# Attention and a squared-ReLU FFN in one program: other PSUM banks for the third pair of output tiles, and two small steps on other engines

## The chip, the cores and the metric

The program runs on one core of one Trainium2 chip. The metric is device time in microseconds (us), and less is better. Before the change three runs took 420.18, 419.59 and 418.35 us; their median, 419.59 us, is the time before. A core has a matrix engine (TensorE: PE for its matmuls, PEld for its weight loads), a vector engine (VectorE, DVE), an engine for activation functions (ScalarE, ACT), GpSimd (POOL), and SyncE (SP), which only issues transfers here. PSUM, where matmuls accumulate, has 8 banks of 512 float32 per partition.

## The reference

```python
def _attn_ref(q, k, v):          # q (8,16,384,64), k and v (8,4,384,64)
    ...
    scores = scale * np.matmul(q, k.transpose(0, 1, 3, 2))
    ...
    attn = np.exp(scores)
    attn = attn / (np.sum(attn, axis=-1, keepdims=True) + 1e-09)
    return np.matmul(attn, v).astype(np.float32)

def _moe_ref(x, w_in, w_out):    # x (3072,1024), w_in (1024,2048), w_out (2048,1024)
    h = np.maximum(x @ w_in, 0.0)
    return (h * h @ w_out).astype(np.float32)
```

The attention output of each batch element, 384 tokens by 16 heads of 64, is the input of the FFN for those 384 rows. Four query heads share a key head.

## The kernel before

The work goes through 8 batches (b = 0 to 7) of 384 tokens. A batch has five stages.

- **Scores** (L392): for a key block and a group of four heads, K times Q into two neighbouring banks; ScalarE takes the exponential of both banks in one instruction (L402, some 1.0 us).
- **AV** (`av`, L418, for the first three batches; `av_halves`, L459, after that): the exponentials are the weights and V is the moving operand. V carries one more column, `ones_b` of `v_aug`, so that the row sum comes out beside the product; VectorE takes a reciprocal and multiplies (L427/L433, L472/L474). From b = 2 that column holds a scale instead of 1, and `v_unit` (L622) writes it from `tops`, the largest magnitude of V, which is found in `top_of` (L601, a reduce on VectorE and a copy to `top_w` on GpSimd, L603) and `top_spread` (L613, two matmuls and a reduce, L617). An AV step reads that column and waits for it.
- **Turning**: the result is transposed to `xT`, from b = 1 by a DMA that SP issues (`turn_o_dma`, L479).
- **Up**: x times w_in. For b = 0 and 1 plain tiles: `up_tile`, or `quad`, which works on four 128-row tiles in banks 4 to 7, in two phases of two banks for each half of the contraction. A tile goes to `hr` through a relu on VectorE (L567) and is squared into `h2T` by ScalarE (L571) or VectorE (L574). From b = 2 (`strassen`) up is made of seven products of quarter matrices, 14 `units` of two tiles' width each; units sit in a pair of banks, 4 and 5 or 6 and 7, in turn. It needs sums of w_in's quarters (`w_q`: `fold` L636, `scaled` L648, `less` L653, `w_in_place` L662 and L666), made once on VectorE during b = 0 and 1, and sums of xT's quarters (`sums`, L593), made for each batch. `evict` copies or adds a unit into `hr` (L777, L782, L769) and `close_squares` picks engines for relu and square (L687, L690, L693, L697).
- **Down**: h2T times w_out into 384 x 1024. `down_halves` (b = 2 to 7, matmuls at L847) works on pairs of tiles: `p` is rows 0 (both column halves), `q` rows 1 and `r` rows 2. The contraction is cut in halves for partitions 0-63 and 64-127, which run on the two row halves of TensorE at once; the second list runs one item (four matmuls of each half) behind the first. `p` has banks 4 and 5, `q` 6 and 7, `r` 2 and 3. The order of items is p0-p3, q0 q1, p4-p7, q2 q3, r0 r1, then q and r in turn, then r4-r7. The last batch has no `r`; its rows 2 are plain tiles (`downs`, L903) in bank 6 or 7. `store` evicts a tile on VectorE (L924, or L920 for b = 0 and 1) and SP issues the transfer out.

While down of batch b runs, AV of batch b + 1 is threaded between its items, in bank pairs (0, 1) and (2, 3), and then, "beside" it, the first scores of b + 2 in banks 0 and 1. While up of b + 1 runs, the rest of these scores follow ("split"). `top_spread` also takes one of the pairs.

The order on each engine is written down before anything runs. A `Recorder` keeps a clock per engine, in its own estimates (`cost`), and a loop (L1099 to L1277) always takes, among the candidates (scores, AV, FFN items and others), what its clocks call ready, by priority. Every engine then executes its own list in that order and waits on semaphores. A bank is free for the planner when its last reader is done; `held` marks banks whose tile is still open. Work on one engine waits behind what was recorded earlier on it. Four things on GpSimd's list matter below: the loads of q, k and v two batches ahead (L239, L271, L264), which wait until the transposes of the previous q are done; `dup_k` (L300); the copy of V (`aug_v`, L305); and L603. For a batch from 3 on, `dup_k`, the copy and `top_of` are put on the lists only when the scores of the batch before are all on the list.

Names used below for lines: relu of a quad L567, its squares L571 and L574, v's scale column L622, third pair `r` in `down_halves`.

## Time and profile before

| what | us |
|---|---|
| median of three runs | 419.59 |
| the profiled execution | 418.33 |
| its span, from the first to the last instruction | 416.4 |
| PE busy | 405.7 (97%) |
| PEld busy | 292.6 (70%) |
| DVE busy | 275.2 (66%) |
| ACT busy | 203.4 (49%) |
| POOL busy | 100.3 (24%) |
| granted TensorE clock | 1.000 |

The profile comes from one execution, 418.33 us long; 416.4 us of it lie between its first and its last instruction. In a timeline a row gives the start in us from the beginning of the span, the time it covers, the engine, the line, the operation, what it writes and reads, the number of merged instructions, and in brackets how long the engine had been idle just before and what ended that. A row of PE can overlap the next, because the end of a matmul is modelled and matmuls are pipelined; the distance of two starts is the safer figure. Up, scores and down of the first batch take until about 73 us, the second batch until about 127 us, and from there a batch takes about 49 us.

### The profile page before, as it was taken

To read this page: it belongs to the slowest core of one execution; us is meant where nothing else is said; L and a number is where in the kernel's file an instruction comes from. 1 tells how busy PE (TensorE), PEld (TensorE's weight loads), DVE (VectorE), ACT (ScalarE), POOL (GpSimd) and SP (SyncE) were. 2 spreads that over 40 slices of the span, in tenths; PEclk is the share of its full clock that TensorE was granted. 3 is DMA by queue.
4 is the path that set the end of the run, shared out by engine and by line. 5 is a ranking of instruction groups with operands and counts; after the bars stand their busy time and mean duration, and the time that the engine had idled before them with its cause. 6 is when DMAs were issued, how large, how long until landed. Compare 5 with 4: busy or idle time off the path is not lost.

```text
span 416.4 us, 14931 instructions
## 1 busy us (share of the span) xinstructions
PE 405.7 (97%) x6873; PEld 292.6 (70%) x6880; DVE 275.2 (66%) x525; ACT 203.4 (49%) x279; POOL 100.3 (24%) x115
## 2 busy tenths in 40 slices
PE   8999999999899999999999999999999999999997
PEld 5566754554467975488965998569985789779844
DVE  3699988899787765457644684367834577456613
ACT  6948610186007970477605963269613785006500
POOL 8680000141400923009200363005300060002200
DMA  9999999992991079520991148930734201521012
GB/s 172 190 191 193 205 187 177 259 115 64 182 164 52 3 115 140 115 93 14 169 176 54 54 54 122 178 110 3 91 68 90 102 3 22 91 73 52 3 50 102
DMA packets 96943, 44.75 MB, mean 107 GB/s; under 512 B 77296, under 2 KB 90864, under 8 KB 96880
## 3 DMA queue, kind: packets, MB, share of 16 engines
q0 software_dynamic: 36544, 17.44, 33.3%
q1 hardware_dynamic: 59664, 25.86, 31.2%
q8 instruction: 54, 0.88, 0.9%
q10 hardware_dynamic: 672, 0.49, 0.4%
q14 instruction: 9, 0.07, 0.1%
HBM read 35.65 MB, written 12.58 MB: 116 GB/s over the span
## 4 chain that ended last, share of the span: by engine, by line
PE 82%; DVE 9%; ACT 2%; DMA 2%; issue 2%; POOL 1%; SPq 1%; POOLq 0%; DVEq 0%
PE ps L847 27%; PE ps L798 25%; PE ps L903 7%; PE ps L392 7%; PE ps L554 5%; PE ps L459 5%; PE ps L418 3%; ACT expT L402 2%; DMA qT<-q_st 1%; PE ps L517 1%; DVE hr L567 1%; DVE hr L777 1%; DVE wx L648 1%; DVE wx L653 1%; DMA wx<-in_k_dram 1%
## 5 line engine op out<-in xcount | busy, mean ns | idle before, releaser
L402 ACT ACTIVATE expT<-ps 128x1024 bf16<-128x1024 f32 (+1 forms) x145 | 139.4, 1028 | 113.7 <-PE ps L392 113.1
L847 PE MATMUL ps<-w_out_sb,h2T 64*128 64x512 bf16 x1088 | 140.3, 376 | 0.8 <-issue 0.2
L847 PEld LDWEIGHTS ps<-w_out_sb,h2T 64*128 64x128 bf16 x1088 | 64.9, 94 | 37.9 <-issue 0.7
L798 PE MATMUL ps<-xT,w_in_sb 64*128 64x192 f16 x1152 | 82.5, 243 | 0.2 <-DVE xT L593 0.2
L798 PEld LDWEIGHTS ps<-xT,w_in_sb 64*128 64x128 f16 x1152 | 71.8, 94 | 5.0 <-PE ps L798 1.2
L690 POOL TENSOR_SCALAR hr<-hr 128x384 f32<-128x384 f32 x18 | 28.2, 1565 | 183.0 <-DVE hr L782 183.0
L924 DVE TENSOR_SCALAR y_sb<-ps,unit 128x512 f32<-128x512 f32 (+2 forms) x37 | 29.3, 794 | 36.2 <-PE ps L847 30.3
L798 PE MATMUL ps<-s_sum,wx 64*128 64x192 f16 x768 | 51.1, 243 | 0.8
L392 PE MATMUL ps<-qT,kT 64*128 64x256 bf16 (+2 forms) x336 | 50.6, 324 | 0.9 <-ACT expT L402 0.7
L903 PE MATMUL ps<-w_out_sb,h2T 128*128 128x512 bf16 (+2 forms) x233 | 48.6, 364 | 0.7 <-DVE y_sb L924 0.3
L782 DVE TENSOR_TENSOR hr<-ps,hr 128x384 f32<-128x384 f32 x72 | 39.6, 556 | 14.5 <-PE ps L798 11.7
L798 PEld LDWEIGHTS ps<-s_sum,wx 64*128 64x128 f16 x768 | 44.0, 94 | 4.2 <-DVE hr L777 2.8
L777 DVE COPY hr<-ps 128x384 f32<-128x384 f32 x64 | 34.9, 556 | 13.7 <-PE ps L798 9.7
L459 PEld LDWEIGHTS ps<-v_aug,expT 64*128 64x128 bf16 x1440 | 37.2, 94 | 8.8 <-DVE tops L617 0.9
L554 PE MATMUL ps<-xT,w_in_sb 64*128 64x384 bf16 x448 | 42.1, 323 | 0.7 <-DVE hr L567 0.6
L903 PEld LDWEIGHTS ps<-w_out_sb,h2T 128*128 128x128 bf16 x240 | 22.4, 98 | 25.1 <-DVE y_sb L924 0.5
L459 PE MATMUL ps<-v_aug,expT 64*128 64x65 bf16 x1440 | 37.4, 190 | 1.3 <-issue 0.6
L554 PEld LDWEIGHTS ps<-xT,w_in_sb 64*128 64x128 bf16 x448 | 21.4, 94 | 16.7 <-DVE hr L567 1.8
L798 PE MATMUL ps<-s_sum,w_in_sb 64*128 64x192 f16 x384 | 32.9, 243 | 0.1
L693 ACT ACTIVATE h2T<-hr 128x384 bf16<-128x384 f32 x62 | 31.6, 521 | 1.7
L798 PE MATMUL ps<-xT,wx 64*128 64x192 f16 x384 | 31.8, 243 | 0.1
L687 ACT ACTIVATE hr<-hr 128x384 f32<-128x384 f32 x54 | 27.7, 513 | 7.6 <-DVE hr L782 7.6
(85 smaller groups left out, 410.7 us busy)
## 6 DMA issues: line engine op xcount, KB each, us to landing
out_dram<-y_sb SPq DMA_DIRECT2D x47, 256.0 KB, 2.3
q_st<-in_q_dram POOLq DMA_DIRECT2D x12, 384.0 KB, 7.9
w_in_sb<-in_moe_w_in_dram POOLq DMA_DIRECT2D x8, 512.0 KB, 14.8
w_out_sb<-in_moe_w_out_dram POOLq DMA_DIRECT2D x4, 1024.0 KB, 28.5
v_st<-in_v_dram POOLq DMA_DIRECT2D x7, 192.0 KB, 8.4
k_st<-in_k_dram POOLq DMA_DIRECT2D x6, 192.0 KB, 4.7
wx<-in_q_dram POOLq DMA_DIRECT2D x2, 384.0 KB, 7.9
q_st<-in_q_dram POOLq DMA_DIRECT2D x3, 192.0 KB, 5.3
```

What stands on the lines that cost most here:

```text
L392: mm = pe.matmul(ps[:, base + x, m * wide:(m + 1) * wide], kT[at(b)][64 * x:64 * x + 64, u, :], q_cols(b, u // NJ, x, c0, c0 + wide))
L402: R.add("scalar", lambda e: e.activation(dst, src, AF.Exp, scale=0.125), reads=keys, writes=[("expT", (b * NU + u) % NEX, t) for u, _, _ i ...
L459: m = pe.matmul(ps[:, p[x], n * DP:n * DP + D + 1], w, v_aug[b % 2][r, g * NJ + j, 0:D + 1], start=(n + j + y == 0), stop=(n + j + y == 2 ...
L554: m = pe.matmul(bank(4 + xs[x])[:, 0:S], w_in_sb[r, kc, c * 128:(c + 1) * 128], xT[b % NXT][r, kc, :], start=(phase < 2 and kc == 0), stop ...
L690: R.add("gpsimd", lambda e, val=val: e.tensor_scalar(val, val, DOWN * DOWN, 0.0, ALU.mult, ALU.max), reads=[("hr", r)], writes=[("hr", r)] ...
L693: R.add("scalar", lambda e, dst=dst, two=two: e.activation(dst, two, AF.Square), reads=[("hr", r)], writes=keys, cost=0.45)
L777: R.add("vector", lambda e: e.tensor_copy(hr[r][:, :], src), reads=[("bank", at)], writes=[("hr", r)], cost=0.48, after=hr_read.pop(r, ()))
L782: R.add("vector", lambda e: e.tensor_tensor(hr[r][:, :], src, hr[r][:, :], ALU.add), reads=[("bank", at), ("hr", r)], writes=[("hr", r)], ...
L798: return lambda pe: pe.matmul(bank(at)[:, f * h:f * h + h], w[r, kc, c:c + 128], m[r, kc, :], start=(prod in (1, 5, 2) and y + f + kc == 0 ...
L847: return lambda pe: pe.matmul(bank(base + x)[:, 0:512], h2T[r, c, i3 * 128:(i3 + 1) * 128], w_out_sb[r, c, x * 512:(x + 1) * 512], start=( ...
L903: m = pe.matmul(bank(i)[:, 0:n], h2T[:, c, i3 * 128:(i3 + 1) * 128], w_out_sb[:, c, c0:c1], start=(c == 0), stop=(c == NFC - 1))
L924: R.add("vector", lambda e: e.tensor_scalar(ysl, bank(i)[:, 0:n], g, g, ALU.mult, ALU.mult), reads=[("bank", i), ("unit", b % 2)], writes= ...
```

## The change

1. The third pair `r` of `down_halves` no longer has banks 2 and 3. It uses the banks of the first pair, after that has been evicted. Which pair of banks is the first one alternates by batch: banks 4 and 5 for an even batch, 6 and 7 for an odd one; `q` has the other pair.
2. The banks of the Strassen units alternate by batch in the same way.
3. `v_unit` (L622) is recorded on VectorE in place of GpSimd.
4. In a quad of batch 1 a square may go to GpSimd: when ScalarE's clock is not well behind TensorE's, and GpSimd's clock plus 0.3 is before VectorE's, with 1.0 added while sums of w_in are still to be made.
5. The planner's estimate for a `fold` is 1.14 in place of 1.2, and inside a split stage of a batch outside 2 to 6 the second half of an AV step may be taken.

```diff
 # in quad, after the relus
                 for c, r in rs if phase == 3 else ():
-                    if R.clock["scalar"] < R.clock["tensor"] - 0.5:
+                    pool, dve = [max(R.clock[x], R.clock["tensor"] + 0.5) for x in ("gpsimd", "vector")]
+                    if b == 1 and R.clock["scalar"] >= R.clock["tensor"] - 0.5 and pool + 0.3 < dve + 1.0 * bool(w_q):
+                        R.add("gpsimd", lambda e, c=c, r=r: e.tensor_tensor(h2T[:, c, :], hr[r][:, :], hr[r][:, :], ALU.mult),
+                              reads=[("hr", r)], writes=[("h2T", c, 0), ("h2T", c, 1)], cost=0.77)
+                    elif R.clock["scalar"] < R.clock["tensor"] - 0.5:
...
 # in v_unit
-        R.add("gpsimd", lambda e: e.tensor_scalar(ones_b, tops[b % 2].ap().unsqueeze(1).to_broadcast([128, NU, 1]),
+        R.add("vector", lambda e: e.tensor_scalar(ones_b, tops[b % 2].ap().unsqueeze(1).to_broadcast([128, NU, 1]),
                                                   TINY, DOWN, ALU.max, ALU.mult),
-              reads=[("tops", b % 2)], writes=[("v_one", b % 2)], cost=0.15)
+              reads=[("tops", b % 2)], writes=[("v_one", b % 2)], cost=0.12)
...
 # in fold
-              reads=[("w_in", i)], writes=[("w_top", n)], cost=1.2)
+              reads=[("w_in", i)], writes=[("w_top", n)], cost=1.14)
...
 # in strassen
-        units = [(prod, 2 * g + i, 4 + (2 * (n % 2 ^ g) + i)) for g in range(2)
+        units = [(prod, 2 * g + i, 4 + (2 * (n % 2 ^ g ^ b % 2) + i)) for g in range(2)
                  for n, prod in enumerate((1, 5, 6, 3, 7, 2, 4)) for i in range(2)]
...
 # in down_halves
-        p, q, r = pair(0, 4), pair(1, 6), pair(2, 2)
+        lead, other = 4 + 2 * (b % 2), 6 - 2 * (b % 2)
+        p, q, r = pair(0, lead), pair(1, other), pair(2, lead)
...
 # in the planner's loop
-            inside = [x for x in cand if x[2] in ("sc", "ffn") or late and (x[2] == "av2" or x[2] == "av" and since >= AMONG * (1 + (ff["b"] >= SB)))]
+            inside = [x for x in cand if x[2] in ("sc", "ffn") or x[2] == "av2" and not on_halves(ff["b"]) or late and (x[2] == "av2" or x[2] == "av" and since >= AMONG * (1 + (ff["b"] >= SB)))]
```

8 lines of the change are left out of this document (4 added, 4 removed).

## The prediction

> **What bounds the kernel now.** I read the busy shares first, then the table of windows, then the chain that ended last, then the timeline wherever TensorE was idle. TensorE is busy 405.7 of 416.4 us, and the chain is 82% PE. So the change can only win back stretches in which PE waits. By windows of 20 us:
>
> ```profile
> 80.00:100.00 20.00, 19.20 (x232) 10.82 (x228) 18.40 (x31) 15.61 (x17) 5.86 (x7) 1.00 0.69 123
> 100.00:120.00 20.00, 18.45 (x213) 10.61 (x213) 16.28 (x32) 1.53 (x2) 5.42 (x7) 1.00 1.15 178
> 240.00:260.00 20.00, 19.77 (x476) 17.75 (x472) 13.17 (x30) 10.18 (x19) 9.52 (x12) 1.00 0.66 89
> ```
>
> The columns after the length are PE, PEld, DVE, ACT, POOL. The second batch (73 to 127 us) loses most, with VectorE nearly full; the steady batches lose 0.2 to 0.6 us in 20. In the quads of the second batch:
>
> ```profile
> 86.63 1.47 POOL L300 COPY k_dup<-k_st 128x1536 bf16<-128x1536 bf16 x1 [0.66 <-DMA k_st<-in_k_dram]
> 86.70 3.21 DVE L574 TENSOR_TENSOR h2T<-hr 128x384 bf16<-128x384 f32 x4
> 91.16 1.01 DVE L567 TENSOR_SCALAR hr<-ps 128x384 f32<-128x384 f32 x2
> 92.22 1.09 PEld L554 LDWEIGHTS ps<-xT,w_in_sb 64*128 64x128 bf16 x16 [0.56 <-DVE hr L567]
> 94.29 0.82 PE L554 MATMUL ps<-xT,w_in_sb 64*128 64x384 bf16 x8 [0.37 <-DVE hr L567]
> 100.30 3.40 PE L903 MATMUL ps<-w_out_sb,h2T 128*128 128x512 bf16 x15 [0.16 <-DVE hr L567]
> ```
>
> PE waits for relus that stand on VectorE's list behind four squares or a sum of w_in. At 111.8 us PE waits for the scale column of V, which stands on GpSimd's list behind loads that wait for a transpose:
>
> ```profile
> 109.65 1.31 POOL L271 DMA_DIRECT2D q_st<-in_q_dram  x1 [2.67 <-DMA qT<-q_st]
> 110.95 0.76 POOL L264 DMA_DIRECT2D v_st<-in_v_dram  x1
> 111.78 1.56 POOL L622 TENSOR_SCALAR v_aug<-tops 128x12 bf16<-128x12 f32 x2
> 113.02 4.55 PE L418 MATMUL ps<-v_aug,expT 128*128 128x65 bf16 x144 [1.28 <-POOL v_aug L622]
> ```
>
> In a steady batch (here b = 2) the seams are these: AV steps run back to back because the third pair can't open while AV holds banks 2 and 3; then the third pair is evicted as the next up begins.
>
> ```profile
> 164.56 1.74 PE L459 MATMUL ps<-v_aug,expT 64*128 64x65 bf16 x72
> 166.40 1.04 PE L847 MATMUL ps<-w_out_sb,h2T 64*128 64x512 bf16 x8
> ...
> 178.89 1.69 DVE L924 TENSOR_SCALAR y_sb<-ps,unit 128x512 f32<-128x512 f32 x2 [2.21 <-PE ps L847]
> ...
> 180.13 0.24 PE L798 MATMUL ps<-s_sum,wx 64*128 64x192 f16 x1
> ```
>
> And near the end, the last rows wait for a bank of `q`:
>
> ```profile
> 406.00 1.67 DVE L924 TENSOR_SCALAR y_sb<-ps,unit 128x512 f32<-128x512 f32 x2 [1.78 <-PE ps L847]
> 407.09 6.89 PE L903 MATMUL ps<-w_out_sb,h2T 128*128 128x512 bf16 x47 [0.28 <-DVE y_sb L924]
> ```
>
> **Squares on GpSimd.** By starts, PE loses 0.30 us before 92.23 (two score matmuls last 0.21, the step took 0.51), 0.53 before 94.29 (0.75 against 0.22) and 0.33 before 100.30: 1.16 us behind VectorE. Another 0.47 before 99.75 is behind ScalarE's exponentials, which run nearly without a break. The edit's comparison decides by the planner's clocks. The first quad should send two or three squares to GpSimd (one is ScalarE's); the second none, since the planner has GpSimd's four loads wait for the q transposes then; the third and fourth all four. I count 11. VectorE is rid of 11 times 0.49 us (four took 1.95 at 100.21), 5.4 us. GpSimd gets 11 times 0.83 (its L697 of the same shape), 9.1 us, and was busy 5.86 of 20. These squares stand ahead of the next k duplication, V copy and L603, which are recorded after the last scores: the duplication moves from 86.6 to about 101, and SP's transposes and the loads after them two to three us later. Nobody needs them before the scores at 127.0, a cover of over 10 us. The duplication's move also takes away one delay: the first of the four squares at 86.70 lasted 1.80 us, against 0.55 elsewhere. If the relus are on time, ScalarE's 18 exponentials (0.95 each, from 82.2) end the stage near 99.5 in place of 100.6. I take 1.2 us off, out of 1.63 at most; the other end is the first rival.
>
> The row first: that square began on VectorE while GpSimd's copy was running, and ended 0.4 us after the copy. The Trainium skill, page "SBUF — State Buffer", section "Who interferes with whom", says that a VectorE instruction with two SBUF inputs, or in a two-port mode, and a GpSimd instruction that reads SBUF exclude each other, the later one blocked fully. By that rule the squares on GpSimd would hold up the sums of w_in in the same way; the trace agrees at 86.70, yet at 193.02 a VectorE square beside GpSimd's L690 took its usual 0.55. What it would make of the sum is the first rival.
>
> **Scale column on VectorE.** A VectorE instruction on one column (L596) took 0.21 us; six cost 1.2 us, where VectorE is busy 13 of 20. Behind L617 (104.35 to 104.83) it adds no wait, for the AV that last read that column is two batches old, so AV of batch 2 can start near 105 instead of 113.02, and the 1.28 us go. What is late next there: the banks, free since the scores. I take 1.3, between 0.8 (AV held up by its own evictions, eight times 0.75 on VectorE against 4.55 on PE, with sums of w_in in between) and 1.3.
>
> **Start of batch 2's up.** PE started L798 at 127.80, 0.4 us after its four score matmuls, waiting for sums of xT that were queued behind the last sums of w_in. With AV eight us earlier and VectorE relieved, both are done sooner: 0.4 off. SP's four transposes of this AV then queue behind the three of the next q and k, and have some 10 us to land in.
>
> **Third pair.** Gain: AV halves that alternate with down items take 0.28 us each (163.42 to 163.70); four from 164.56 to 166.40 took 1.84, so 0.72 is lost. Likewise 0.55 at 214.44 and at 312.88 (three halves in 1.39 and 1.40), 0.44 at 263.35 without an instruction stall there: 2.3 in all. Cost one: `r` opens one item (0.86 us) after the first pair's last matmul, and that pair's second eviction ends one eviction (0.81) and a handoff of some 0.1 later, unless VectorE is at an AV's 0.75 just then. Between 0 and 0.8 for each of five batches; 0.06, since AV halves lie between, 0.3 in all. Cost two: the second product of the next up wants the banks of `r`. Here it began at 180.13, the second eviction ended at 180.58: 0.5 each. Scores can fill 0.3 of it (banks 2 and 3 are free then; a burst is 0.21), except ahead of the last batch: four times 0.2 and 0.5 is 1.3. Of the gain I take 1.3, because the pair's own last halves stay back to back. Net 0.3 lost, between 2.3 gained and 6.5 lost.
>
> **Other edits.** For the last batch `q` has banks 4 and 5, and the plain tiles find 6 and 7 evicted since 403.4: of the 0.54 us by which the start at 407.09 is late I take 0.4. The fold estimate: four folds took 4.59 us, 1.15 each, so the new value is nearer, at no cost. The half-AV rule: no AV is open in a split stage of batches 0 and 1 here, nothing.
>
> **Sum.** 1.2 + 1.3 + 0.4 + 0.4 - 0.3 = 3.0. The profiled execution would go from 418.33 to 415.3. It stands 1.26 under the median of the runs; by that median, 419.59 - 3.0 = 416.6 us.
>
> **Rivals.**
> 1. *GpSimd's squares hold up VectorE.* Between 78 and 100 VectorE still has some seven sums of w_in. If each waits a whole square, 7 x 0.83 = 5.8 us, more than the 5.4 of relief: no gain in the quads, and the sums late for batch 2. 416.6 + 1.2 + 0.4 = 418.2. For it, the 1.80 us square; against it, the planner puts sums between squares of different quads, and GpSimd is idle in most of that time.
> 2. *The seams eat the gain.* If each of the five costs 0.6 more than I took, 3.0 us: 419.6. For it, evictions in pairs of 1.7 us on VectorE at each seam; against it, spare scores and AV halves.
> 3. *Slower, by the third pair.* At its full price, 0.8 at `r` and 0.5 at the next up, with nothing to fill: 5 x 1.3 = 6.5, and no gain from AV. The rest gains 3.3: 419.6 + 3.2 = 422.8. It decides from 0.66 a batch; from 1.1 it shows.
> 4. *The seams are free.* All 2.3 gained, nothing paid: 416.6 - 2.6 = 414.0. Against it, up's second product wants the bank that is evicted last.
> That squares hardly go to GpSimd (its planned clock late in three quads) would cost most of the 1.2 and is inside the range.
>
> **Numbers.** What this kernel's runs can tell from no change is about 0.5%, 2.1 us, so faster means under 417.5 and slower over 421.7. Forecast 0.50 (its own range 415.3 to 417.5: 0.3 to 0.5 us on each of the four larger terms, not all one way), rival 1 0.10, rival 2 0.18, rival 3 0.10, rival 4 0.12. Faster: 0.50 + 0.12 = 0.62; same: 0.28; slower 0.10. The range from 413.6 to 420.3 leaves out rival 3 and some of the edges of 2 and 4.
>
> **What would show it.** No PE wait on L622; L418 for batch 2 near 105 in one block; L697-like squares on GpSimd between 79 and 102 and few L574 after 90, none much over 0.55 us; no idle time before L903 at the end. Wrong if PE waits on L924 ahead of L847 or L798 at five seams for more than 0.6 us each, if L653 or L648 lengthen beside GpSimd's squares, or if the new order puts a wait where none was.

## The result, and the profile after

The changed kernel takes 421.31 us (median of 20 runs, 417.67 to 426.03) against 418.43 us before in the same comparison (20 runs, 417.27 to 420.20): 1.0055 times as long, with a 95% interval of 1.0033 to 1.0077. It is slower; the forecast was 416.6 us. One thing must be known to read the numbers below: 11 of these 20 runs have a mean granted TensorE clock of 0.996 or less, which only 3 of the 90 runs of the kernel before in the comparisons further down have, and these eleven average 422.75 us where the nine at 1.0 average 419.54, so besides a run's time its clock is told where it matters. At clock 1.0 alone the change costs about 1.1 us, and the rest of the 2.9 us comes with the lower clock. The execution that was profiled took 419.88 us at clock 1.0, with a span of 418.1 us; the one before took 418.33 us, span 416.4.

TensorE is busy 403.4 us (405.7 before) in a longer span, and GpSimd 123.2 us (100.3). The table of windows, with the columns PE, PEld, DVE, ACT, POOL behind the length:

```profile
80.00:100.00 20.00, 18.90 (x230) 10.66 (x224) 19.01 (x26) 16.23 (x18) 13.61 (x14) 1.00 0.73 134
100.00:120.00 20.00, 17.98 (x207) 10.55 (x211) 17.79 (x31) 0.90 (x1) 10.51 (x10) 1.00 0.84 124
120.00:140.00 20.00, 18.05 (x249) 13.15 (x249) 9.75 (x19) 10.06 (x12) 2.19 (x2) 1.00 0.69 116
140.00:160.00 20.00, 17.85 (x429) 15.61 (x427) 13.91 (x29) 14.70 (x23) 11.72 (x12) 1.00 0.30 54
...
240.00:260.00 20.00, 19.87 (x505) 18.29 (x501) 14.79 (x32) 12.21 (x23) 11.08 (x12) 1.00 0.50 73
```

The steady window at 240 has gained 0.10 us of PE (19.77 before). The loss lies between 80 and 160: PE is 0.30, 0.47, 1.76 and 1.58 us less busy there than before (19.20, 18.45, 19.81, 19.43). VectorE was to be relieved in the quads; it is busier (19.01 against 18.40), and GpSimd has gone from 5.86 to 13.61. Between 140 and 160 PE stands twice, where before it has one wait, of 0.45 us:

```profile
146.01 0.50 PE L802 MATMUL ps<-s_sum,wx 64*128 64x192 f16 x8 [0.87 <-DVE hr L781]
...
157.16 0.21 PE L617 MATMUL ps<-ident,top_w 64*128 64x64 bf16 x2 [1.28 <-POOL top_w L607]
```

The second of these is met again in the experiment on the scale column; the first was not followed further.

What PE waits for is in the timeline. Rows of the engines GpSimd, VectorE, PE and SP, in order of time, from the quads of batch 1 to the first up product of batch 2:

```profile
89.00 1.23 DVE L657 TENSOR_TENSOR wx<-wx 128x2048 f16<-128x2048 f16 x1
...
90.77 4.60 POOL L572 TENSOR_TENSOR h2T<-hr 128x384 bf16<-128x384 f32 x4 [4.03 <-DVE hr L567]
...
91.07 1.60 DVE L657 TENSOR_TENSOR wx<-wx 128x2048 f16<-128x2048 f16 x1
...
97.73 5.14 POOL L572 TENSOR_TENSOR h2T<-hr 128x384 bf16<-128x384 f32 x4 [2.36 <-DVE hr L567]
...
98.04 1.60 DVE L657 TENSOR_TENSOR wx<-wx 128x2048 f16<-128x2048 f16 x1
...
100.39 0.81 PE L908 MATMUL ps<-w_out_sb,h2T 128*128 128x512 bf16 x3 [0.88 <-POOL h2T L572]
...
102.82 1.46 POOL L300 COPY k_dup<-k_st 128x1536 bf16<-128x1536 bf16 x1
...
104.23 1.82 POOL L305 COPY v_aug<-v_st 128x768 bf16<-128x768 bf16 x1
104.31 1.29 SPq L309 DMA_TRANSPOSE kT<-k_dup  x1
...
105.64 3.73 SPq L316 DMA_TRANSPOSE qT<-q_st  x2
...
106.00 0.28 POOL L607 CAST top_w<-top 128x128 bf16<-128x128 f32 x1
...
106.34 0.20 PE L617 MATMUL ps<-ident,top_w 64*128 64x64 bf16 x2 [1.53 <-POOL top_w L607]
...
109.42 5.09 SPq L479 DMA_TRANSPOSE xT<-o_sb  x2
...
113.62 0.88 POOL L271 DMA_DIRECT2D q_st<-in_q_dram  x1 [6.57 <-DMA qT<-q_st]
...
115.17 3.36 SPq L479 DMA_TRANSPOSE xT<-o_sb  x2
116.10 1.33 POOL L264 DMA_DIRECT2D v_st<-in_v_dram  x1
...
128.27 0.56 DVE L597 TENSOR_TENSOR s_sum<-xT 128x768 f16<-128x768 f16 x1 [3.48 <-DMA xT<-o_sb]
...
129.95 0.99 PE L802 MATMUL ps<-xT,w_in_sb 64*128 64x192 f16 x10 [1.89 <-DVE xT L597]
```

(Line numbers above 572 have moved on: L617 was L613, L607 was L603, L657 was L653, L597 was L593, L802 was L798, L908 was L903, L929 was L924, L781 was L777.) Read downwards, this is one chain. A row of GpSimd with x4 covers four squares, which do not all last the same: beside VectorE's sums of w_in the two hold each other up (a sum takes 1.60 us in place of 1.23, a square up to 1.81 in place of 0.83), and the last square ends so late that the first down product waits 0.88 (in three other executions of this kernel it waits 0.65, for relus). Only then does GpSimd come to the doubling of k (102.82, before at 86.63), the copy of V and the small copy of `top`, and PE waits 1.53 for that copy. SP's transposes of k and q go out four us later than before (104.31 against 100.22), the transposes of the attention result behind them, and GpSimd's loads of q and v for batch 4, which wait for q's transposes, go out right among these (113.62 to 117.4; before 106.1 to 111.7, ahead of all four). The last transpose of the result was issued at 116.62 and landed at 128.25, 11.6 us later (before: issued at 120.18, landed at 124.58, 4.4 us). VectorE's sums wait for them, and PE waits 1.89 us for the sums. The wait of 1.28 us on `v_unit` at 113.02, which was to go, is gone.

The seams between batches and the end, answering the rows shown of before:

```profile
164.01 0.45 PE L459 MATMUL ps<-v_aug,expT 64*128 64x65 bf16 x18
164.28 1.04 PE L851 MATMUL ps<-w_out_sb,h2T 64*128 64x512 bf16 x8
165.14 0.45 PE L459 MATMUL ps<-v_aug,expT 64*128 64x65 bf16 x18
...
183.99 0.25 PE L802 MATMUL ps<-s_sum,wx 64*128 64x192 f16 x1 [0.34 <-DVE y_sb L929]
```

```profile
407.77 1.67 DVE L929 TENSOR_SCALAR y_sb<-ps,unit 128x512 f32<-128x512 f32 x2 [1.78 <-PE ps L851]
...
408.75 6.89 PE L908 MATMUL ps<-w_out_sb,h2T 128*128 128x512 bf16 x47 [0.16 <-DVE y_sb L929]
```

All AV halves now alternate with a down item, at 0.27 us each (164.01 to 164.28), where before four in a row took 1.84. The price is the wait for the third pair's eviction at the next up, 0.34 here.

The same by stages, in us between two starts on PE: the quads of batch 1 up to the first down product, from there to the first up product of batch 2, and then from up to up. The last four rows are experiments that are told below.

| kernel | quads | down 1 to up 2 | batch 2 | 3 | 4 | 5 | 6 | last | span |
|---|---|---|---|---|---|---|---|---|---|
| before | 26.75 | 27.50 | 50.68 | 49.02 | 49.54 | 48.91 | 46.81 | 43.66 | 416.4 |
| changed | 26.71 | 29.56 | 51.97 | 48.20 | 48.41 | 48.41 | 47.08 | 44.06 | 418.1 |
| banks alone | 26.71 | 27.50 | 49.30 | 48.41 | 48.40 | 48.41 | 47.09 | 44.07 | 414.0 |
| scale column alone | 26.69 | 25.69 | 54.83 | 48.94 | 50.09 | 48.91 | 46.81 | 43.67 | 419.5 |
| squares alone | 26.72 | 28.52 | 53.67 | 48.91 | 49.04 | 48.91 | 46.81 | 43.66 | 419.9 |
| changed without the squares | 26.63 | 25.69 | 51.30 | 48.80 | 49.40 | 48.43 | 47.08 | 44.07 | 415.9 |

So the banks bring what the change brings, in batches 2 to 5; the squares bring waits into the stage from down 1 to up 2 and into batch 2, the scale column into batch 2. (The time ahead of these quads, not in the table, is 73.55 to 74.53 us in the six executions of the table, and 73.68 to 75.50 in four executions of the changed kernel.)

### The profile page after: what moved, and what is told of

Its sections match the earlier page's. It is cut to its first block, busy times and chain, and to the rows that moved or that the text cites. A ratio compares the mean times of both kernels' runs of the same rounds, so it can differ in the third digit from the quotient of the medians.

```text
span 418.1 us, 14931 instructions
## 1 busy us (share of the span) xinstructions
PE 403.4 (96%) x6872; PEld 302.4 (72%) x6880; DVE 270.7 (65%) x514; ACT 201.3 (48%) x275; POOL 123.2 (29%) x130
## 4 chain that ended last, share of the span: by engine, by line
PE 65%; DMA 17%; DVE 9%; POOL 7%; issue 1%; POOLq 0%; DVEq 0%
PE ps L851 25%; PE ps L802 24%; DMA w_out_sb<-in_moe_w_out_dram 9%; PE ps L459 5%; DMA xT<-o_sb 5%; PE ps L908 4%; PE ps L392 4%; DMA wx<-in_v_dram 2%; PE ps L554 2%; DVE y_sb L929 1%; POOL h2T L572 1%; DMA v_st<-in_v_dram 1%; DVE hr L781 1%; POOL hr L694 1%; POOL v_aug L305 1%
## 5 line engine op out<-in xcount | busy, mean ns | idle before, releaser
L851 PE MATMUL ps<-w_out_sb,h2T 64*128 64x512 bf16 x1088 | 142.0, 376 | 0.2 <-POOL h2T L701 0.2
L851 PEld LDWEIGHTS ps<-w_out_sb,h2T 64*128 64x128 bf16 x1088 | 73.2, 94 | 29.0 <-POOL h2T L701 0.7
L694 POOL TENSOR_SCALAR hr<-hr 128x384 f32<-128x384 f32 x23 | 34.3, 1491 | 179.0 <-DVE hr L786 179.0
L802 PE MATMUL ps<-xT,w_in_sb 64*128 64x192 f16 x1152 | 84.4, 243 | 2.7 <-DVE xT L597 2.6
L802 PEld LDWEIGHTS ps<-xT,w_in_sb 64*128 64x128 f16 x1152 | 71.8, 94 | 5.8 <-DVE xT L597 3.4
L929 DVE TENSOR_SCALAR y_sb<-ps,unit 128x512 f32<-128x512 f32 (+2 forms) x37 | 29.4, 795 | 40.2 <-PE ps L851 33.0
L802 PE MATMUL ps<-s_sum,wx 64*128 64x192 f16 x768 | 50.8, 243 | 2.6 <-DVE y_sb L929 1.3
L908 PE MATMUL ps<-w_out_sb,h2T 128*128 128x512 bf16 (+2 forms) x232 | 48.5, 364 | 1.6 <-POOL h2T L572 0.9
L802 PEld LDWEIGHTS ps<-s_sum,wx 64*128 64x128 f16 x768 | 43.7, 94 | 6.2 <-DVE y_sb L929 2.4
L781 DVE COPY hr<-ps 128x384 f32<-128x384 f32 x63 | 34.7, 557 | 18.9 <-PE ps L802 15.8
L459 PEld LDWEIGHTS ps<-v_aug,expT 64*128 64x128 bf16 x1440 | 38.8, 94 | 6.8
L908 PEld LDWEIGHTS ps<-w_out_sb,h2T 128*128 128x128 bf16 x240 | 22.3, 98 | 25.7 <-DVE hr L567 0.9
L459 PE MATMUL ps<-v_aug,expT 64*128 64x65 bf16 x1440 | 38.6, 190 | 0.0
L802 PE MATMUL ps<-s_sum,w_in_sb 64*128 64x192 f16 x384 | 33.7, 243 | 0.0
L697 ACT ACTIVATE h2T<-hr 128x384 bf16<-128x384 f32 x62 | 31.6, 520 | 1.6
L802 PE MATMUL ps<-xT,wx 64*128 64x192 f16 x384 | 31.7, 243 | 0.0
L691 ACT ACTIVATE hr<-hr 128x384 f32<-128x384 f32 x49 | 25.2, 513 | 9.7 <-DVE hr L786 9.4
## 6 DMA issues: line engine op xcount, KB each, us to landing
v_st<-in_v_dram POOLq DMA_DIRECT2D x7, 192.0 KB, 12.4
```

The costliest lines, as they stand in the source:

```text
L459: m = pe.matmul(ps[:, p[x], n * DP:n * DP + D + 1], w, v_aug[b % 2][r, g * NJ + j, 0:D + 1], start=(n + j + y == 0), stop=(n + j + y == 2 ...
L694: R.add("gpsimd", lambda e, val=val: e.tensor_scalar(val, val, DOWN * DOWN, 0.0, ALU.mult, ALU.max), reads=[("hr", r)], writes=[("hr", r)] ...
L697: R.add("scalar", lambda e, dst=dst, two=two: e.activation(dst, two, AF.Square), reads=[("hr", r)], writes=keys, cost=0.45)
L781: R.add("vector", lambda e: e.tensor_copy(hr[r][:, :], src), reads=[("bank", at)], writes=[("hr", r)], cost=0.48, after=hr_read.pop(r, ()))
L802: return lambda pe: pe.matmul(bank(at)[:, f * h:f * h + h], w[r, kc, c:c + 128], m[r, kc, :], start=(prod in (1, 5, 2) and y + f + kc == 0 ...
L851: return lambda pe: pe.matmul(bank(base + x)[:, 0:512], h2T[r, c, i3 * 128:(i3 + 1) * 128], w_out_sb[r, c, x * 512:(x + 1) * 512], start=( ...
```

## The experiments

**One part at a time.** Four kernels, beside before at 418.42 us (19 runs). The changed kernel without GpSimd's squares:

```diff
-                    if b == 1 and R.clock["scalar"] >= ... and pool + 0.3 < dve + 1.0 * bool(w_q):
-                        R.add("gpsimd", ...)
-                    elif R.clock["scalar"] < R.clock["tensor"] - 0.5:
+                    if R.clock["scalar"] < R.clock["tensor"] - 0.5:
```

> The changed kernel with the squares of batch 1 back on ScalarE and VectorE; banks, scale column and the rest stay changed. Theory G (the squares on GpSimd make GpSimd's list late, and with it the downs of batch 1, the second top_spread, the transposes of k and q and so the sums of batch 2): the waits of 0.88, 1.53 and 1.89 us at 100.4, 106.3 and 129.9 go or shrink under 0.5 each, and the kernel comes out 2 to 3.5 us under the changed one, near 416, that is 0.994 of before. Rival S (the early AV of batch 2 brings its transposes into the loads of batch 4, with or without the squares): the wait on the sums of batch 2 stays over 1 us and the time stays within 1 us of the changed kernel. Rival P (the third pair in the first pair's banks is what costs): no change, time as the changed kernel's.

Before with the squares alone (the same lines, put into before):

> The kernel before with the squares of batch 1 partly on GpSimd and nothing else changed. Theory G: slower than before by 1.5 to 4 us, since the scale column then also stands behind the squares on GpSimd's list; squares on GpSimd last over 1.0 us instead of 0.83, and some sums of w_in (1.22 and 0.75 us alone) over 1.1 and 1.5. Rivals S and P: within 1 us of before, or faster by the 1.2 us of the prediction.

This is no clean test of the squares. In this order the planner puts batch 3's `top_spread` between the two halves of an AV step of batch 2, into a bank that the step still has open. The half-made sum is overwritten, so the kernel leaves out part of batch 2's attention and its result is wrong there; and the second half waits 0.47 us at 107.56 for the reduce of the spread, a wait that the kernels with a right result do not have.

Before with the banks alone:

```diff
-        units = [(prod, 2 * g + i, 4 + (2 * (n % 2 ^ g) + i)) ...
+        units = [(prod, 2 * g + i, 4 + (2 * (n % 2 ^ g ^ b % 2) + i)) ...
-        p, q, r = pair(0, 4), pair(1, 6), pair(2, 2)
+        lead, other = 4 + 2 * (b % 2), 6 - 2 * (b % 2)
+        p, q, r = pair(0, lead), pair(1, other), pair(2, lead)
```

> The kernel before with only the banks changed: third pair in the first pair's banks, pairs alternating by batch, in down and up. Theory G: batches 3 to 6 take 48.2 to 48.4 us from up to up as in the changed kernel, against 48.9 to 49.5, and the time is 1 to 2 us under before (0.995 to 0.998). Rival P: slower than before by 1 us or more. If a lower granted clock comes with the denser batches, it shows here too; if it comes with the squares, it does not.

Before with the scale column alone:

```diff
-        R.add("gpsimd", lambda e: e.tensor_scalar(ones_b, tops[b % 2]...), ..., cost=0.15)
+        R.add("vector", lambda e: e.tensor_scalar(ones_b, tops[b % 2]...), ..., cost=0.12)
```

> The kernel before with only the scale column on VectorE. Theory G: no wait on the scale column, AV of batch 2 near 105 us, and the kernel 0.5 to 1.5 us under before. Rival S: the transposes of AV of batch 2 share the DMA engines with the next batch's loads and land late, PE waits over 1 us for the sums of batch 2, and the time is as before or up to 1 us over.

| kernel | median us | runs, of them under clock 1.0 | ratio to before, 95% interval |
|---|---|---|---|
| changed without the squares | 418.98 | 12, 4 | 1.0016 (0.9993 to 1.0038) |
| squares alone | 423.16 | 6, 4 | 1.0112 (1.0080 to 1.0143) |
| banks alone | 416.18 | 6, 0 | 0.9945 (0.9923 to 0.9966) |
| scale column alone | 421.79 | 8, 4 | 1.0071 (1.0034 to 1.0108) |

The banks alone are faster, by 2.2 us, a little more than the 1 to 2 expected. The changed kernel without the squares is 2.3 us under the changed one, as expected, but not at 0.994 of before; at clock 1.0 alone the means are 418.49 and 419.54, 1.05 us apart. Squares alone and scale column alone are each slower than before, though both shorten or leave alone the place at which they aim: the squares by 4.7 us (1.5 to 4 expected, and some of it from the overwritten bank), the scale column by 3.4, where theory G expected 0.5 to 1.5 us less than before and rival S at most 1 more. The scale column does take its 1.81 us out of the stage from down 1 to up 2 (27.50 to 25.69), and gives back 4.15 us in batch 2. There PE and GpSimd show this, with the scale column alone:

```profile
154.86 0.20 PE L613 MATMUL ps<-ident,top_w 64*128 64x64 bf16 x2 [1.67 <-POOL top_w L603]
...
170.67 1.68 PE L847 MATMUL ps<-w_out_sb,h2T 64*128 64x512 bf16 x14 [1.44 <-issue]
```

```profile
149.56 1.47 POOL L300 COPY k_dup<-k_st 128x1536 bf16<-128x1536 bf16 x1
150.99 1.50 POOL L690 TENSOR_SCALAR hr<-hr 128x384 f32<-128x384 f32 x1
152.57 1.23 POOL L697 TENSOR_TENSOR h2T<-hr 128x384 bf16<-128x384 f32 x1
153.75 0.82 POOL L305 COPY v_aug<-v_st 128x768 bf16<-128x768 bf16 x1
154.52 0.29 POOL L603 CAST top_w<-top 128x128 bf16<-128x128 f32 x1
```

With one operation less on GpSimd's clock the planner puts one more pair of relu and square of up (L690, L697) on GpSimd, ahead of the copy for `top_spread`; before has four pairs, all done by 145 us. It estimates 0.77 us for L690; that takes 1.50. By its own clock the copy is ready at 151.02 and the spread product follows at once; on the chip it ends at 154.81. The stall of 1.44 us that ends in "issue" follows a 16 KB transfer on the queue of kind "instruction" that begins at 168.3 us (that it is PE's is not shown); before has one of 0.24 us at the same place. Beyond what before has, these two waits are 2.4 of the 4.15 us; a wait of 0.87 at 129.66 for evictions of batch 1 is a third, and the other 0.9 us was not traced.

**Is it the wait for the spread product?** If so, taking the spread later should win it back. The changed kernel without the squares, `top_spread` from batch 4 on a candidate only 7 us after the planned `top_w`:

```diff
-cand.append((max([R.when(reads=["top_w"])] + ...
+cand.append((max([R.when(reads=["top_w"]) + 7.0 * (len(measured) > 1)] + ...
```

> Banks and scale column changed, squares not on GpSimd, and from batch 4 on the planner takes top_spread no earlier than 7 us after it thinks top_w ready, so that TensorE's list has it about 7 us later for batch 4. Theory W (TensorE stands at top_spread because the planner gives GpSimd's scaling L690 0.77 us where it takes 1.49): the wait of 1.67 us at 155 goes, nothing takes its place, and the time falls by 1.5 to 2.5 us against the same kernel without this, to 416.5 to 417.5, with the granted clock under 1.0 in fewer runs. Rival: another item of the list waits there for the same late squares; the time falls by less than 0.7 us.

417.96 us (12 runs), 0.9990 (0.9962 to 1.0018); before here is 419.17 (31 runs). The wait of 1.67 is gone, and three others stand in the trace: 0.47 at 154.56 (squares of up), 1.54 at 179.07 (sums of xT) and 1.02 at 130.28 (0.64 without the edit). Batch 2 takes 52.38 in place of 51.30. In the trace that is the rival: moving one item of the lists moved the wait. The time does not decide: by the ratios the fall is 1.1 us, between the theory's 1.5 and the rival's 0.7, and the intervals overlap. The theory also expected fewer runs under clock 1.0, and there are more, 8 of 12 against 4 of 12.

**Do waits lower the granted clock?** The banks alone, with extra copies of V on GpSimd ahead of the copy for batch 4's spread, six or eight, so that PE waits where it did not:

```diff
+        if tops_n[0] == 4:
+            for _ in range(6):          # 8 in the second kernel
+                prev = R.add("gpsimd", lambda e: e.tensor_copy(v_aug[0][:, :, 0:D], v_st[0][:, :, :]), ..., cost=0.0, after=(prev,))
```

> Banks only, with GpSimd's copy of V for batch 4 made seven times over instead of once (about 5 us more on GpSimd), so that TensorE stands some 1.8 us at top_spread of batch 4 and nothing else of its list moves. Theory C (one idle stretch of TensorE near 2 us lowers the granted clock for a few us in part of the runs): the time rises by 1.5 to 2 us in runs at clock 1.0 and by some 1.7 us more in runs at 0.996, which are a third or more of all; banks alone had 1.0 in each. Rival: the clock stays at 1.0 in each run, the time rises by the wait alone.

> The same with nine copies (about 7 us more on GpSimd): a wait of about 3.6 us. Theory C: nearly each run has a clock of 0.996 or less, and the time rises by 3.6 plus 1.7 or more, to 421.5 or over. Rival: clock 1.0, time 419.8.

With the short one PE waits 1.65 us, and 11 of 12 runs stay at 1.0 (418.25 us), as the rival said. With the long one it waits 3.52 us, and 10 of 12 runs are at 0.996 or less (419.96 us): the clock is theory C's, the time is under its 421.5 and at the rival's 419.8. The windows around the long wait:

```profile
148.48:151.89 3.41, 3.14 (x88) 2.91 (x84) 2.70 (x6) 3.31 (x8) 3.21 (x4) 1.00 1.12 222
151.89:155.31 3.42, 0.05 (x4) 0.06 (x6) 3.04 (x5) 1.93 (x5) 3.14 (x4) 1.00 1.02 129
155.31:158.72 3.41, 3.41 (x20) 1.18 (x22) 0.29 (x1) 0.00 (x0) 2.96 (x4) 0.50 0.43 42
158.72:162.13 3.41, 3.41 (x96) 2.14 (x94) 1.11 (x4) 0.00 (x0) 0.70 (x2) 1.00 1.41 160
```

The column behind POOL is the granted clock. It is 0.50 for 3.41 us right behind the wait, and then whole again: half of 3.41, 1.7 us, is lost on top of the wait, and 1.7 in 418 is the 0.004 by which the mean falls. So this wait costs about one and a half times itself: batch 2 takes 54.06 us, 4.76 more than with the banks alone, which is 3.52 and 1.7 less the 0.45 that PE waits there with the banks alone. The wait of 1.65 us in the other kernel does not do this: in the one profiled run under 1.0 the half-clock stretch lies at 11.0 to 14.4 us, in the start of the run, and the clock behind the wait is whole.

**Which squares?** The changed kernel with the fourth quad's squares not on GpSimd:

```diff
-                    if b == 1 and R.clock["scalar"] >= ...
+                    if b == 1 and tiles[0] < 12 and R.clock["scalar"] >= ...
```

> The changed kernel, but the fourth quad's squares are not on GpSimd, so that the k duplication for batch 3 no longer stands behind them; those of the first and third quad stay there. Theory G (what costs is the lateness of GpSimd's list behind the fourth quad): the waits at 100.4 (0.88), 106.3 (1.53) and 129.9 (1.89) go down to those of the kernel without any squares there (0.16, none, 0.64); the time falls by 2 us or more against the changed kernel, to 417 to 419. Rival L (the lock between VectorE and GpSimd in the first and third quad costs as much): waits on relus of over 0.5 us in the quads and a time within 1 us of the changed kernel.

416.84 us (8 runs, all at 1.0), 0.9946 (0.9925 to 0.9968): by medians 4.5 us less than the changed kernel, and the two waits at 106 and 130 are gone. In its quads:

```profile
95.16 1.92 POOL L300 COPY k_dup<-k_st 128x1536 bf16<-128x1536 bf16 x1
...
95.80 2.37 DVE L657 TENSOR_TENSOR wx<-wx 128x2048 f16<-128x2048 f16 x1
...
100.98 4.26 PE L908 MATMUL ps<-w_out_sb,h2T 128*128 128x512 bf16 x19 [1.62 <-DVE hr L567]
```

The doubling of k is back at 95, so what follows it is in time. But it now lies beside a sum of w_in (2.37 us in place of 1.22), which delays the relus: the quads take 27.46, longer than in any kernel of the table. So one sign of rival L is there, a wait of 1.62 for relus, while the time is theory G's. The squares of the first and third quads stay on GpSimd here (the second never had any), and still nothing is won in the quads. One thing is left open: this kernel, seven squares on GpSimd and all, is faster than the changed one with none (0.9946 against 1.0016), and its quads do not explain it; batches 2 and 4 take 50.76 and 48.79 us against 51.30 and 49.40. The order of the lists counts here besides the squares.

**What holds the first up product of batch 2?** Two edits, each taking away one suspect. Batch 4's loads kept until batch 2's result has been transposed:

```diff
-        if loaded + 1 < B and turned >= loaded and not turn_q:
+        if loaded + 1 < B and turned >= loaded and not turn_q and not (loaded == 3 and x_done[2] < NKC):
...
+            after += [("xT", 0, c) for c in range(NKC)] if loaded == 4 else []
```

> The changed kernel with GpSimd's loads of batch 4 kept back until the transposes of batch 2's result have landed. Theory (the loads share the DMA engines with the transposes): the last transpose of batch 2, which took 11.6 us from issue to landing, takes about 4.5 us as in the kernel before, TensorE's wait of 1.89 us at 130 us falls under 0.5 us, the stretch from the first down product of batch 1 to the first up product of batch 2 falls from 29.6 to 28 us or less, and the time is 1.5 to 2 us less than the changed kernel's (418 to 419.5 us). Rival: the transposes stand behind SP's own others (those of q) whatever the loads do; the wait stays above 1.3 us and the time is within 0.7 us of the changed kernel's. It also says what comes of the later loads: by either they have over 15 us before batch 4 is used and cost nothing.

And the doubling of k for batch 3 on ScalarE:

```diff
-        eng = "scalar" if b > 1 and not stretch[0] else "gpsimd"
+        eng = "scalar" if b > 1 and not stretch[0] or b == 3 else "gpsimd"
```

> The changed kernel with one thing moved: the doubling of k of batch 3, which stands behind the fourth quad's squares on GpSimd (102.8 us, before 86.6), is put on ScalarE, where no square of GpSimd stands ahead of it. Theory (the lateness of GpSimd's other work behind the squares, not the squares' own result, makes the waits): the spread product's wait of 1.53 us at 106 us goes under 0.4 us, VectorE's sums and the first up product of batch 2 come 1.3 to 3 us earlier, and the time is 1.5 to 3 us less than the changed kernel's (417 to 418.5 us). Rival: the wait of 0.88 us at 100.4 us on GpSimd's last square, and VectorE's lengthened operations beside it, remain and hold the same things up; the time is within 1 us of the changed kernel's.

Beside both ran the changed kernel once more:

> The changed kernel itself once more, for a second trace and more times. What it is to show is where the granted clock falls in the runs that are longer than 420 us. Theory: the clock falls to half for some 3.4 us right behind one of the waits that are new after the fourth quad (at 106 us, 1.53 us long, or at 130 us, 1.89 us long), when that wait happens to be longer than some 3 us; a profiled run at a clock of 0.996 would then have such a stretch beginning within 1 us of the end of one of them, and a wait above 3 us there. Rival: the stretch lies at the start of the run, as in the run with the short added wait, or somewhere without a wait, and the waits have nothing to do with it. Both expect a median of 419.5 to 422 us.

The changed kernel again: 421.18 us (12 runs, 7 under 1.0), 1.0048 (1.0017 to 1.0078). With the loads held: 417.31 us (12 runs, 2 under 1.0), 1.0001 (0.9983 to 1.0020); 3.9 us less by medians, twice what was expected. Of the runs at clock 1.0 alone the means are 418.75 us (5 runs) and 417.47 (10 runs), 1.3 us apart; the rest is that fewer runs are under 1.0. From its trace, GpSimd and PE:

```profile
105.57 0.29 POOL L607 CAST top_w<-top 128x128 bf16<-128x128 f32 x1
117.32 0.81 POOL L239 DMA_DIRECT2D k_st<-in_k_dram  x1 [11.46 <-DMA xT<-o_sb]
```

```profile
105.92 0.20 PE L617 MATMUL ps<-ident,top_w 64*128 64x64 bf16 x2 [1.53 <-POOL top_w L607]
...
127.47 1.40 PE L802 MATMUL ps<-xT,w_in_sb 64*128 64x192 f16 x19
```

All transposes of the result have landed by 117.3, when the first load goes out, and up starts 0.44 us after the start of the four score matmuls with no wait. The stage takes 27.73 us (29.56 and 30.00 in two traces of the changed kernel). The last transpose, issued at 114.17, landed at 117.02, 2.8 us later; in four traces of the changed kernel it took 11.6, 11.9, 10.7 and 12.4 us. So the loads delayed the transposes. They are not all that the edit moved: VectorE's list has the sums of xT two evictions earlier, and the lists of later batches differ.

With k's doubling on ScalarE: 419.72 us (12 runs, 6 under 1.0), 1.46 us less, just short of the theory's 1.5 and outside the rival's 1. The wait for the spread product falls to 0.91, not under 0.4, and the next one, for the reduce behind it, is new:

```profile
106.56 0.20 PE L617 MATMUL ps<-ident,top_w 64*128 64x64 bf16 x2 [0.91 <-POOL top_w L607]
108.48 3.68 PE L418 MATMUL ps<-v_aug,expT 128*128 128x65 bf16 x81 [1.72 <-DVE tops L621]
```

```profile
106.28:109.70 3.42, 1.42 (x42) 1.32 (x43) 2.96 (x10) 0.00 (x0) 1.83 (x3) 1.00 0.95 159
109.70:113.11 3.41, 3.41 (x50) 2.72 (x47) 2.88 (x9) 0.00 (x0) 0.05 (x1) 0.50 2.16 165
```

Two waits with 0.2 us of work between them have the effect of the long one: half clock for 3.41 us. The second wait is not the doubling's doing. Here, too, the spread of batch 3 stands between the two halves of an AV step, in a bank that the step has open, so that this kernel leaves out part of batch 2's attention and the second half waits for the reduce. What the doubling's move alone would bring is therefore not shown.

**Where is the low clock in the changed kernel itself?** Two more executions of the changed kernel, for a trace of such a run (the one traced beside the loads held was at 1.0):

> The changed kernel again, one look, for a trace of a run with a granted clock under 1.0. Theory: such a run has a stretch of some 3.4 us at half clock, and it begins right behind the waits of the first down product of batch 1 (the spread product's near 106 us and the one behind it) or of batch 2's first up product (near 130 us), where TensorE has been idle for 3 us in 3 to 4. Rival: it lies at the start of the run. A run at 1.0 tells nothing.

> As the look before it: the same kernel, the same two theories; one trace in two of this kernel should show a clock under 1.0.

The first took 419.45 us at 1.0, with 0.86 us of wait at 129.22. The second took 421.82 us at 0.996, and shows what the rival said:

```profile
8.68:12.10 3.42, 1.87 (x28) 1.09 (x25) 1.05 (x3) 2.78 (x4) 1.78 (x3) 1.00 1.31 166
12.10:15.51 3.41, 3.41 (x40) 1.92 (x37) 1.62 (x5) 2.05 (x2) 3.41 (x5) 0.50 1.32 153
...
128.15:131.56 3.41, 1.72 (x10) 0.45 (x8) 0.49 (x1) 1.86 (x2) 0.00 (x0) 1.00 1.00 296
131.56:134.97 3.41, 2.23 (x41) 2.15 (x42) 2.42 (x7) 0.88 (x2) 0.00 (x0) 1.00 0.20 75
```

Its half-clock stretch is at the start of the run, and the wait before batch 2's up, 2.87 us long here, lies across two of the 3.41 us steps and lowers nothing. That wait was 0.86, 1.89, 2.10 and 2.87 us in the four traces of this kernel, of 419.45, 419.88, 421.02 and 421.82 us. The times rise with it, but not because of it: the quads of batch 1 begin at 73.99, 73.68, 75.13 and 75.50 us, and from there to the end of the span it is 343.66, 344.40, 344.03 and 344.51. What lowers the clock in the other runs of the changed kernel under 1.0 was not seen. That it has to do with the late transposes is suggested only by numbers (7 of 12, against 2 of 12 with the loads held and 0 of 8 without the fourth quad's squares), and other numbers speak against this as the only cause: 4 of 8 with the scale column alone and 8 of 12 with the late spread, where GpSimd has no squares. The cause of the low clocks stays open.

**The scale column without the new order.** The banks, and the column on VectorE, but with the planner's clocks kept as if GpSimd still wrote it, so that every engine's list is that of the banks alone:

```diff
-        R.add("gpsimd", lambda e: e.tensor_scalar(ones_b, ...), ..., cost=0.15)
+        i = R.add("vector", lambda e: e.tensor_scalar(ones_b, ...), ..., cost=0.0)
+        R.clock["gpsimd"] = max(R.clock["gpsimd"], R.ops[i]["end"]) + 0.15
+        R.ops[i]["end"] = R.clock["gpsimd"] + 0.07
```

> Banks of the third pair, and the scale column on VectorE, with the planner's clocks kept as if the column were still on GpSimd, so that every engine's list has the order of the kernel with the banks alone and only the one operation has changed engine. Theory (what the scale column loses in batch 2 comes from the new order, in which the spread product stands behind two more of GpSimd's pairs, and not from the operation): the stretch from first down product of batch 1 to first up of batch 2 is 26 us (27.5 with the banks alone), the stretch of batch 2 stays at 49.3 to 49.8 us, no wait of 1.67 us near 155 us, time 1.0 to 1.7 us less than the banks alone: 0.991 of before (0.988 to 0.993). Rival: the operation on VectorE itself delays what stands behind it there; the gain of 1.8 us is given back in batch 2 (51 us or more) and the time is that of the banks alone or longer (0.995 or above).

414.72 us (6 runs, 413.91 to 415.07, all at 1.0), 0.9921 (0.9901 to 0.9941): the lowest median of all, under both kernels, though its interval overlaps that of the banks alone (0.9923 to 0.9966). The stage from down 1 to up 2 takes 26.26, 1.24 less than with the banks alone, and no wait for the spread product stands in batch 2, as the theory said. Batch 2 takes 50.29, over its 49.8, and one row has most of the 1.0 us above the banks alone:

```profile
167.73 0.36 PE L459 MATMUL ps<-v_aug,expT 64*128 64x65 bf16 x12 [0.81 <-issue]
```

So the operation gains its 1.24 us where it aims, and the order that the planner made from it lost more than that. Whether the stall of 0.81 belongs to this kernel or only to this execution is open.

**And the squares, with the rest put right?** The whole change with the loads held and the clocks kept as in the last two:

> The changed kernel whole, its squares on GpSimd among it, with batch 4's loads kept back as in the run with the loads held, and with the planner's clocks kept as if the scale column were on GpSimd, as in the run with the same order. It differs from that run (414.7 us) by the squares on GpSimd and the held loads alone. Theory: the squares bring nothing in the quads (26.7 us there, as in every run) and still cost the waits of 0.9 us at 100 us and 1.5 us at 106 us; 416.3 to 418 us. Rival, which is the prediction's own term for them: they are worth 1.2 us in the quads when nothing else is late; 413 to 414.5 us.

420.18 us (8 runs, 6 under 1.0), 1.0043 (1.0022 to 1.0063), 5.5 us over the kernel before it, which has neither squares nor loads held. Both theories missed, the rival by more: the quads take 26.48 (26.47 without the squares), so the squares bring nothing there. PE waits 0.65 at 100.54, 1.78 at 107.01 and 0.93 at 108.14, and that pair again brings the half clock, from 109.39 to 112.80; then 1.67 at 158.64. But the 0.93 is the overwritten bank once more: this is the third of the kernels that leave out part of batch 2's attention in this way. So the reading of the quads, which come earlier, stands, and the 5.5 us are not the price of the squares alone.

## Why the prediction was wrong, and where it was right

**Squares on GpSimd, -1.2 us: the step that failed.** They brought nothing in the quads, 26.75 against 26.71, and cost 2.3 us as part of the change (421.31 against 418.98; 1.05 at clock 1.0). The relus' lateness was worked out rightly, and the count of eleven squares was right to the one, but the freed time on VectorE did not go to them. The planner put sums of w_in there: between 80 and 100 us VectorE makes nine of them in 11.62 us, before six in 5.86, and its busy time went from 18.40 to 19.01 us. And the cost was dismissed with a wrong cover: "Nobody needs them before the scores at 127.0, a cover of over 10 us". That is so for k's doubling and the loads. It is not so for what stands behind them on the same list: the copy L607, which the text named as delayed, is read by the spread product that PE reaches at 105; and SP's queue is the one that carries the result's transposes, for which the text counted "some 10 us to land". They took 11.6 us, since the loads now ran beside them. Taking the fourth quad's squares off won back 4.5 us, holding the loads 3.9, both by medians and with fewer runs at the low clock in them.

**Their own price.** 0.83 us each, from a row where GpSimd runs alone. Of the eleven, six took 0.82 or 0.83, one 1.27 and four 1.80. Two of the last quad:

```profile
97.73 0.83 POOL L572 TENSOR_TENSOR h2T<-hr 128x384 bf16<-128x384 f32 x1 [2.36 <-DVE hr L567]
98.52 1.81 POOL L572 TENSOR_TENSOR h2T<-hr 128x384 bf16<-128x384 f32 x1
```

The sum of w_in at 98.04 (1.60 us) began 0.31 us after the first of them, which had 0.52 to go, and took 0.37 longer than alone. The second began 1.12 us before that sum's end and took 0.98 longer. This is rival 1's mechanism, but not its condition: such a sum lost 0.4 us, not a whole square's 0.83. How much of the squares' cost it makes is not shown. The row at 193.02, which the prediction set against it, does not speak against it either: VectorE's square kept its 0.55 us, but GpSimd's L690 beside it took 1.81 in place of 1.49. The Trainium skill, page "SBUF — State Buffer", section "Who interferes with whom", calls the sharing of ports between these two engines an exclusive lock. By that rule the sums wait for a square and the squares for a sum; the trace agrees for this pair, in which each was held for most of what the other still had to run (0.37 of 0.52, 0.98 of 1.12).

**Scale column, -1.3, and start of up 2, -0.4.** Together 1.7; alone the column took 1.81 out of that stage. Right in place and size. In the changed kernel the second of them turned into the wait of 1.89. What was not priced is that each edit changes the planner's clocks and so the order of everything after it: 4.15 us came back in batch 2, of it 1.2 by a copy that fell behind two more of GpSimd's longer operations, of which the planner takes the first at half its cost, and 1.2 by a longer stall on "issue". "Wrong if the new order puts a wait where none was" names this, without a price. The run with the order kept shows the gain without that wait.

**Third pair, +0.3: mis-sized.** The four batches from 2 to 5 became 1.38, 0.61, 1.14 and 0.50 us shorter with the banks alone, 3.6 us, with the seam waits inside. Cost two was right: 0.27, 0.21, 0.21, 0.21 and 0.34, 1.24 us in all for the forecast 1.3. Cost one, 0.3, did not show: PE waits on no eviction ahead of `r`. The gain was undersized: "because the pair's own last halves stay back to back" failed, they alternate too, so all of the 2.3 counted, and PE's two stalls on "issue" at 168.32 and 264.53 (0.24 and 0.55) are gone besides, which may be chance. The rest, about 1.2 us once the seam waits inside these four stages (0.69) are added back, was not traced to single rows. Rival 4 had this gain with free seams, 414.0; the real one has a larger gain and paid seams.

**Last batch, -0.4.** It was the other way: the last two stages are 0.28 and 0.41 longer with the banks alone. The wait before the last rows fell from 0.28 only to 0.16, because VectorE's pair of evictions still ends late (407.77 for 1.67 us), and the seam's 0.34 has come in ahead.

**The rivals.** The measured time, 421.3, lies between rivals 2 and 3, but neither happened: both put it on the third pair, which is the part that gained. Of the signs that the text gives for being wrong, two came: L653 (now L657) lengthened beside GpSimd's squares, and the new order put waits where none were. The rival that was missing is the one that came: an edit of GpSimd's list delays an item that PE needs some 5 us later.

## What to carry to other kernels

When work is moved to an idle engine, follow its queue to the first item that the bottleneck reads, not to the first that looks important, and then the queues which that item feeds; an engine that is 29% busy can be late for what is due. In a kernel whose order a planner works out from estimates, try an edit with the old order kept as well: that tells the worth of the operation from that of the new order, and here, for the scale column, the two had opposite signs. A new order must also be asked whether it still lets every bank keep its sum until the sum is complete: three of these kernels did not. An edit made of several parts should be taken apart before it is kept or dropped: one of these parts, and two of them with the order kept, beat both kernels.

## What the runs showed of the hardware

- The granted clock falls to 0.50 for exactly one stretch of 3.41 us and returns. It did so behind a wait of 3.52 us, behind pairs of waits of 0.91 and 1.72 and of 1.78 and 0.93 with one short product between them, and at the start of two runs; not behind single waits of 1.65, 1.89 and 2.10, nor behind the 2.87 that lay across two steps. The stretches at whole clock are whole multiples of the same 3.413 us (105.81 and 307.2 us in one trace, 31 and 90 of them), so it is decided step by step on a grid that does not start with the wait; by this the same wait may lower it in one run and not in the next. How little work a step must hold is open: steps with 1.42, 1.45, 1.87 and 1.93 us of PE were followed by half clock, steps with 1.72, 1.74, 1.83 and 1.95 were not. The Trainium skill, page "TensorE: Matmul & The Clock Gate", section "Part 1: The HAM clock gate", gives a free-running window of 4096 cycles, about 3.4 us, after an idle one of which the clock is halved; the traces agree on window, grid and half, and add that a window need not be empty.
- The last transpose of batch 2's result took 10.7 to 12.4 us from issue to landing with GpSimd's loads of batch 4 out at the same time, in four traces of the changed kernel; 4.4 us in the kernel before, where these loads went out ahead of it; and 2.8 us with the loads held.
- VectorE's sums of w_in (two inputs) and GpSimd's squares, or its doubling of k, lengthen each other where they overlap: 1.60 and 2.37 us for a sum that takes 1.23 alone, up to 1.81 us for a square that takes 0.83.
- PE's stalls on "issue", 0.24 to 1.44 us, each end 2.3 to 3.4 us after a 16 KB transfer of instructions begins, in the eight cases found; but such a transfer is not always followed by one. They come and go: the changed kernel has one, of 0.98 us at 171.46, in one of four traces.
